# Token products on four array quarters, with one table for the order of all steps, in a recurrent-attention kernel

## The chip, the cores and the metric

The kernel runs on one core of one Trainium2 chip. The metric is the device time of one execution in microseconds (us); smaller is better. A run is called slow when it lies over 1.5% above the fastest of the same kernel on its chip; comparisons use the other runs. The medians quoted below are over all runs, slow ones included.

## The reference

A recurrent attention block gives `y`, and a low-rank token mixer with a channel mixer follows. There are 4 batches, 8 heads, 768 tokens and 40 values to a head.

```python
for t in range(S):                       # state: batch x head x 40 x 40
    y[t]  = einsum('bhd,bhde->bhe', r[t], state)
    Sa    = einsum('bhde,bhe->bhd', state, a[t])
    state = state * w[t] - outer(Sa, b[t]) + outer(v[t], k[t])
x  = y as (batch, token, 8 * 40)
u  = x + transpose(transpose(x) @ U @ V)  # token mixer of rank 32
out = u + maximum(u @ w_ch1, 0) @ w_ch2   # channel mixer, 320 -> 1280 -> 320
```

## The kernel before

The kernel cuts the tokens into 12 chunks of 64. Two batches lie on the two halves of the 128 partitions, so there are 2 x 12 = 24 units of work, each with 8 heads. A unit needs the inverse of a triangular 64x64 matrix for each head. Its 32x32 blocks are eliminated as "lanes" on VectorE or GpSimd, stored to DRAM and fetched back. Then `carry` takes the state from one unit to the next.

In `carry`, batch `x` and head slot `s` (heads `2i` and `2i+1`) name the places on the 128x128 array. An input on partition half `x` whose product is written to half `x` is said to use a diagonal quarter only; the trace before shows these products as 64*64, and 32 of them took 1.01 to 1.06 us (lines 606, 629, 678). The state is kept masked by slot in `ST`, so that a product with 128 input rows can pick it up.

```python
hs = [(i, s, x) for i in range(NP) for s in range(2) for x in range(2)]
for i, s, x in hs:                       # value part: diagonal quarters
    nc.tensor.matmul(out=ph[half(x), s, i], lhsT=u.e[half(x), s, i, :],
                     rhs=vt[half(x), 2 * i + s, 0:D], ...)
for i in range(NP):                      # state part: 128 input rows
    for x in range(2):
        nc.tensor.matmul(out=ph[half(x), :, i], lhsT=u.fa[:, i, half(x)],
                         rhs=ST[:, 2 * i + x, :, 0:D], ...)
# ... the same two kinds again for py, with u.cm and u.fr, and with ng for the token sum ...
for h in range(NH):                      # the state turned: 8 full transposes
    nc.tensor.transpose(out=p[:, h // 4, 128 * (h % 4):128 * (h % 4 + 1)],
                        in_=ST[:, h].rearrange("p s e -> p (s e)"), identity=ID[:])
# ... (cut)
# substitute(): one scratch tile with one buffer, whichever engine eliminates
tmp = qp.tile([128, 240], F32, name="tmp")
GR = [[0, 1], [2, 3]] + [list(range(n, n + 4)) for n in range(4, N, 4)]
# ... (cut) the order: a list LEAD of steps for the start, then a list repeated for every slot,
# with rules such as gathers() and lanes() that issue work when it has become possible
```

## Time and profile before

| | us |
|---|---|
| median of the runs before the prediction | 894.96 (891.09 to 895.43) |
| start, until the first token product of unit 0 | 124.2 |
| middle, the 24 units | 470.9 |
| last stage, the channel mixer | 307.0 |

The stages are read from the profile, which was taken in a run of 903.76 us, 9 us above the median.

The prediction below shows how these stages are read. PE is TensorE, DVE VectorE, ACT ScalarE, POOL GpSimd; "L606" is line 606.

### The profile page before, as it was taken

The numbers are of one execution on the slowest core, as the hardware profiler recorded it, in microseconds if no ns is written. First come the engines' busy times: TensorE is split into PE (matmuls) and PEld (weight loads), VectorE is DVE, ScalarE is ACT, GpSimd is POOL, SyncE is SP. The second block draws the span as 40 slices with busy tenths as digits, with TensorE's granted clock in tenths as the row PEclk, the third lists the DMA queues.
The fourth block names the chain that finished last, engine by engine and source line by source line (L and its number), as shares of the span: only waits on it lengthen the run. The fifth ranks groups of instructions, "written<-read, shape, count | busy, mean of one in ns | idle before, by whom it ended". The sixth has DMA issues, their size and how long they took to land.

```text
span 902.1 us, 27425 instructions
## 1 busy us (share of the span) xinstructions
PE 742.7 (82%) x11914; PEld 546.0 (61%) x11914; DVE 395.5 (44%) x794; ACT 265.1 (29%) x660; POOL 287.3 (32%) x532
## 2 busy tenths in 40 slices
PE   3512285874988989978997999989999999999996
PEld 2412174773977878867886877745546364555544
DVE  5556254552465545556659858731011211112010
ACT  2303042632453535535643535411010000001010
POOL 3323732635367167437749444410000000000000
PEclk9999996977697968979987879989999999999999
DMA  4630444243344444445433543200101000000101
GB/s 63 104 65 1 73 89 85 44 84 66 68 71 78 92 82 81 98 77 90 94 71 74 110 111 83 57 12 1 29 1 29 1 15 15 7 23 1 29 2 32
DMA packets 215265, 49.78 MB, mean 55 GB/s; under 512 B 207617, under 2 KB 210721, under 8 KB 215137
## 3 DMA queue, kind: packets, MB, share of 16 engines
q1 hardware_dynamic: 211968, 47.45, 27.7%
q8 instruction: 96, 1.57, 0.7%
q10 hardware_dynamic: 3168, 0.49, 0.4%
q14 instruction: 33, 0.26, 0.1%
HBM read 37.68 MB, written 10.22 MB: 53 GB/s over the span
## 4 chain that ended last, share of the span: by engine, by line
PE 55%; DVE 8%; DMA 4%; POOL 3%; SPq 2%; issue 2%; ACT 1%; DVEq 0%; POOLq 0%; ACTq 0%
PE p L276 14%; PE p L262 12%; PE p L265 4%; PE ph L606 2%; DMA nT<-td 2%; PE px L589 2%; SPq L335 2%; PE pS L687 2%; PE pe L423 2%; PE ph L611 1%; PE py L629 1%; PE pX L620 1%; PE pv L412 1%; PE py L678 1%; DMA td<-ln 1%
## 5 line engine op out<-in xcount | busy, mean ns | idle before, releaser
L276 PE MATMUL p<-ip,hid 128*128 128x320 f32 x384 | 107.3, 432 | 0.0
L520 POOL TENSOR_TENSOR ln<-ln,tmp 128x30 f32<-128x30 f32 (+19 forms) x180 | 97.0, 539 | 14.1
L518 POOL TENSOR_TENSOR tmp<-ln 128x30 f32<-128x30 f32 (+19 forms) x180 | 92.8, 516 | 23.3 <-DVE ln L520 8.6
L262 PE MATMUL p<-uf,W 128*128 128x512 f32 x200 | 93.7, 612 | 0.0
L267 ACT ACTIVATE hid<-p 128x512 f32<-128x512 f32 x30 | 17.9, 597 | 256.3 <-PE p L265 256.3
L276 PEld LDWEIGHTS p<-ip,hid 128*128 128x128 f32 x384 | 73.0, 190 | 30.4
L268 DVE TENSOR_SCALAR hid<-p 128x512 f32<-128x512 f32 x30 | 20.7, 692 | 126.7 <-PE p L265 126.7
L262 PEld LDWEIGHTS p<-uf,W 128*128 128x128 f32 x200 | 36.9, 192 | 51.9 <-issue 51.1
L469 POOL TENSOR_TENSOR nBT<-nB,ip 128x320 f32<-128x320 f32 x24 | 20.8, 865 | 138.3 <-DVE ip L465 76.9
L279 DVE TENSOR_TENSOR o<-p,XTM 128x320 f32<-128x320 f32 x24 | 11.8, 491 | 117.3 <-PE p L276 117.3
L412 PE MATMUL pw<-ID,nWC 128*128 128x128 f32 x96 | 20.7, 352 | 41.7 <-DVE nWC L437 41.6
L465 DVE RECIPROCAL ip<-ip 128x320 f32<-128x320 f32 x24 | 51.7, 2153 | 0.8
L412 PEld LDWEIGHTS pw<-ID,nWC 128*128 128x128 f32 x96 | 13.7, 177 | 44.1 <-DVE nWC L437 18.3
L423 PE MATMUL pe<-fa,fk 64*64 64x64 f32 x768 | 18.2, 238 | 26.9 <-DVE sn L667 26.0
L428 DVE TENSOR_TENSOR ng<-pg,MU 128x512 f32<-128x512 f32 x24 | 16.5, 688 | 49.2 <-PE pg L423 49.2
L606 PE MATMUL ph<-nV,e 64*64 64x40 f32 x768 | 35.9, 263 | 1.9 <-DVE e L428 1.6
L606 PEld LDWEIGHTS ph<-nV,e 64*64 64x64 f32 x768 | 32.8, 174 | 5.6 <-DVE e L428 2.4
L589 PE MATMUL px<-t,GX 32*64 32x32 f32 x768 | 34.2, 241 | 1.6 <-ACT GX L582 1.6
L412 PE MATMUL pk<-ID,nKT 128*128 128x128 f32 x96 | 15.5, 285 | 24.1 <-POOL nKT L542 24.1
L589 PEld LDWEIGHTS px<-t,GX 32*64 32x64 f32 x768 | 31.0, 159 | 6.8 <-ACT GX L582 4.5
L687 PE MATMUL pS<-ID,ST 128*128 128x128 f32 x176 | 28.1, 311 | 7.8 <-ACT ST L674 3.8
L412 PE MATMUL pb<-ID,nBT 128*128 128x128 f32 x96 | 19.1, 333 | 17.5 <-POOL nBT L469 17.5
(168 smaller groups left out, 1482.8 us busy)
## 6 DMA issues: line engine op xcount, KB each, us to landing
raw<-in_moe_w_ch_dram SPq DMA_DIRECT2D x18, 320.0 KB, 3.1
nR<-in_r_dram SPq DMA_DIRECT2D x48, 80.0 KB, 2.9
nK<-in_k_dram SPq DMA_DIRECT2D x48, 80.0 KB, 2.9
nV<-in_v_dram SPq DMA_DIRECT2D x48, 80.0 KB, 3.0
out_dram<-o SPq DMA_DIRECT2D x48, 80.0 KB, 2.0
nW<-in_w_dram SPq DMA_DIRECT2D x46, 80.0 KB, 3.0
nA<-in_a_dram SPq DMA_DIRECT2D x46, 80.0 KB, 2.8
nB<-in_b_dram SPq DMA_DIRECT2D x46, 80.0 KB, 2.9
```

What stands on the lines that cost most here:

```text
L262: nc.tensor.matmul(out=ps_[x][:], lhsT=W1[i][:, (j + x) * 128:(j + x + 1) * 128], rhs=uf[i], start=(i == 0), stop=False)
L265: nc.tensor.matmul(out=ps_[x][:], lhsT=W1[2][half(x), (j + x) * 128:(j + x + 1) * 128], rhs=uf[2][half(x)], start=False, stop=True)
L276: nc.tensor.matmul(out=p[:, 0:DM], lhsT=hid[:, f, 2 * j * L:2 * (j + 1) * L], rhs=W2[f], start=(f == 0), stop=(f == NJ - 1))
L412: nc.tensor.transpose(out=p[:, 128 * i:128 * (i + 1)], in_=t[:, 2 * i:2 * i + 2, :].rearrange("p h e -> p (h e)"), identity=ID[:])
L423: nc.tensor.matmul(out=p[half(z), s, off + DP * i:off + DP * (i + 1)], lhsT=x[half(s), i, half(z)], rhs=y[half(s), i, half(z)], start=True ...
L465: nc.vector.reciprocal(out=u.ip[:], in_=u.ip[:])
L469: nc.gpsimd.tensor_tensor(out=bt[:, :, 0:D], in0=u.nat["B"][:], in1=u.ip[:], op=ALU.mult)
L518: eng.tensor_tensor(out=x, in0=ln[:, 0:j, j:j + 1].to_broadcast([m, j, n]), in1=ln[:, j:j + 1, j + 1:].to_broadcast([m, j, n]), op=ALU.mult)
L520: eng.tensor_tensor(out=ln[:, 0:j, j + 1:], in0=ln[:, 0:j, j + 1:], in1=x, op=ALU.add)
L589: nc.tensor.matmul(out=px[half(x), 32 * h:32 * h + 32], lhsT=GX[s, h, :], rhs=u.t2[s, h, :], start=True, stop=True)
L606: nc.tensor.matmul(out=ph[half(x), s, i], lhsT=u.e[half(x), s, i, :], rhs=vt[half(x), 2 * i + s, 0:D], start=i + s == 0, stop=first, skip_ ...
L687: nc.tensor.transpose(out=p[:, h // 4, 128 * (h % 4):128 * (h % 4 + 1)], in_=ST[:, h].rearrange("p s e -> p (s e)"), identity=ID[:])
```

## The change

The intent is to shorten TensorE's slot. All token products visit the four quarters in turn: slot 1 writes its output to the other half ("crossed"), so its batches have to be swapped back by two half-tile copies per tile. The state is kept unmasked (`SK`), which removes the masked copies; it is turned by 16 small products. Unit 0's lanes are eliminated alone. A second scratch tile parts VectorE from GpSimd. One table, `ORDER`, fixes the order of every step and the queue of every load. PSUM goes from three single and two double banks (and one for `py`) to two single and three double ones.

```diff
-            for i, s, x in hs:
-                nc.tensor.matmul(out=ph[half(x), s, i], lhsT=u.e[half(x), s, i, :], rhs=vt[half(x), 2 * i + s, 0:D],
+            four = [(i, s, x) for i in range(NP) for s, x in ((0, 0), (1, 1), (0, 1), (1, 0))]
+            for i, s, x in four:
+                nc.tensor.matmul(out=pv[half(x ^ s), s, D * i:D * (i + 1)], lhsT=u.e[half(x), s, i, :],
+                                 rhs=vt[half(x), 2 * i + s, 0:D], start=True, stop=True)
+                for i, s, x in four:
+                    nc.tensor.matmul(out=p[half(x ^ s), s, D * i:D * (i + 1)], lhsT=u.fa[half(s), i, half(x)],
+                                     rhs=state["K"][half(s), i, x, 0:D], start=True, stop=True)
+                nc.vector.tensor_tensor(out=rs, in0=ve[:], in1=p[...], op=ALU.subtract)
   ... (cut: the read of the state with SV, the token sums with ng and cm, likewise)
+        def across(eng, u, t):
+            for x in range(2):
+                eng.dma_start(out=u.x[half(x), 1], in_=t[half(1 - x)])
   ... (cut)
-                for h in range(NH):
-                    nc.tensor.transpose(out=p[:, h // 4, 128 * (h % 4):128 * (h % 4 + 1)],
-                                        in_=ST[:, h].rearrange("p s e -> p (s e)"), identity=ID[:])
+                for i in range(NP):
+                    for x in range(2):
+                        for s in range(2):
+                            nc.tensor.matmul(out=p[half(s), 64 * (2 * i + x):64 * (2 * i + x + 1)],
+                                             lhsT=state["K"][half(s), i, x, :], rhs=ID[half(s), half(s)],
+                                             start=True, stop=True)
   ... (cut)
-        GR = [[0, 1], [2, 3]] + [list(range(n, n + 4)) for n in range(4, N, 4)]
+        GR = [[0], [1, 2, 3]] + [list(range(n, n + 4)) for n in range(4, N, 4)]
-                tmp = qp.tile([128, 240], F32, name="tmp")
+                tmp = qp.tile([128, 240], F32, name="tmp" if eng is nc.gpsimd else "tmpv")
-            return ps.tile([128, 512], F32, name=name, tag="one", bufs=3)
+            return ps.tile([128, 512], F32, name=name, tag="one", bufs=2)
-            return ps.tile([128, 2, 512], F32, name=name, tag="two", bufs=2)
+            return ps.tile([128, 2, 512], F32, name=name, tag="two", bufs=3)
   ... (cut: LEAD, the slot list and their rules go)
+        ORDER = """
+W0 W1a B1x A0 V1a f0 A1x B0x p1 f0 W2x q1 f0 A2 f0 K1x f1 q0 f0 f0 R1x f1 f1 w q0 V2 B2x W3x f1 f2 f1 f0 q1 A3x f2
   ... (cut: 45 more such rows; f, s, c are steps of a unit, W A B V R K loads, g gathers, t fetches, l lanes)
```

## The prediction

> **What bounds the kernel now.** I read the page first (busy shares, the 40 slices), then the three stages by windows, then one undisturbed slot on TensorE (PE), then the waits of the start.
>
> The page's busy shares and two rows of its 40 slices:
>
> ```profile
> PE 742.7 (82%) x11914; PEld 546.0 (61%) x11914; DVE 395.5 (44%) x794; ACT 265.1 (29%) x660; POOL 287.3 (32%) x532
> ...
> PE   3512285874988989978997999989999999999996
> ...
> PEclk9999996977697968979987879989999999999999
> ```
>
> PE is the busiest engine, but it is nearly empty in the first five slices and clocked down in many slices of the middle. So there are three stages: a start until the first token product of unit 0 (it begins at 124 us by the row of line 606, whose 24 uses run from 124.2 to 583.3), the 24 units, and the channel mixer from 595 us on. The windows, with these cuts (columns: stretch, its length, busy us of each engine with its count, granted clock, DMA share, GB/s):
>
> ```profile
> 0.00:124.00 124.00, 44.65 (x452) 35.95 (x452) 66.59 (x145) 24.85 (x66) 51.83 (x127) 1.00 0.38 64
> 124.00:595.00 471.00, 401.98 (x10403) 352.81 (x10402) 282.67 (x571) 218.89 (x558) 235.50 (x405) 0.85 0.42 80
> 595.00:902.10 307.10, 296.06 (x1060) 157.24 (x1060) 46.25 (x79) 21.34 (x36) 0.00 (x0) 0.98 0.06 14
> ```
>
> The last stage is solid PE work that the diff doesn't touch: 307 us stay. The middle is PE-led (402 of 471 us), at a mean clock of 0.85. The start is bound by nobody's capacity: VectorE (DVE), its busiest engine, has 66.6 us of work in 124 us.
>
> One slot that ran at full clock without gaps, on PE (start, us until the group's last end, group); I cost a group by the distance to the next start, because neighbours overlap:
>
> ```profile
> 359.77 1.13 PE L629 MATMUL py<-nKT,cm 64*64 64x40 f32 x32
> 360.83 0.77 PE L634 MATMUL py<-S,fr 128*64 128x80 f32 x16
> 361.54 0.66 PE L417 MATMUL pn<-ID,xf 128*128 128x128 f32 x4
> ...
> 365.92 0.65 PE L423 MATMUL pe<-fa,fk 64*64 64x64 f32 x32
> 366.39 0.84 PE L423 MATMUL pe<-fr,fv 64*64 64x64 f32 x32
> 367.02 1.08 PE L678 MATMUL py<-nBT,ng 64*64 64x40 f32 x32
> 368.03 0.69 PE L578 MATMUL pg<-tt,fh 32*32 32x32 f32 x32
> 368.65 1.09 PE L687 MATMUL pS<-ID,ST 128*128 128x128 f32 x8
> 369.67 1.12 PE L589 MATMUL px<-t,GX 32*64 32x32 f32 x32
> 370.72 1.13 PE L606 MATMUL ph<-nV,e 64*64 64x40 f32 x32
> 371.78 0.77 PE L611 MATMUL ph<-ST,fa 128*64 128x80 f32 x16
> 372.49 0.65 PE L412 MATMUL pv<-ID,nV 128*128 128x128 f32 x4
> ...
> 376.22 0.78 PE L634 MATMUL py<-S,fr 128*64 128x80 f32 x16
> ```
>
> The reader is to see two things. The period, 360.83 to 376.22, is **15.4 us**: the PE floor of a slot. And 32 products of 64x64 that visit all four quarters (line 423) take 0.47 us, while 32 on the diagonal quarters (lines 606, 629, 678: input half x, output half x) take 1.01 to 1.06. The real slot is longer: 23 intervals between 124.2 and about 582.4 us give 19.9 us. The excess of 4.5 us is idle time and low clock: the chain of waits shows line 606's group at 1.86 us several times, against 1.06 here.
>
> Waits within the first 124 us on DVE, and in the middle stage (waiter <- releaser: total, times, longest):
>
> ```profile
> DVE tmp L518 <- POOL ln L520: 19.3, 7, 6.8
> DVE nWC L437 <- DMA nW<-in_w_dram: 11.5, 3, 6.5
> ```
> ```profile
> DVE tt L563 <- DMA nT<-td: 48.3, 10, 14.2
> ```
>
> The first is a false dependence: the elimination of units 0 and 1 on DVE and that of units 2 and 3 on GpSimd (POOL) share one scratch tile "tmp" with one buffer, so the engines take turns. The last is the fetch of eliminated lanes arriving too late for the slot.
>
> [...]
>
> **The change part by part.**
> 1. *Token products, per slot on PE.* Removed: 1.06 (606) + 0.71 (611) + 1.06 (629) + 0.71 (634) + 1.01 (678) + 1.02 (eight full transposes, 687) = 5.57 us. Added: five groups of 32 on four quarters (value part, state part, read of the state, and the two token sums). Such groups cost 0.47 to 0.63 in this slot by what follows; I take 0.58: 2.9 us. The state transpose becomes 16 small products on two quarters, at the 33 ns of line 606: about 0.53, with a switch 0.6. Sum 3.5. The floor falls by 2.1 to **13.3 us**.
> 2. *DVE, per unit.* The slot-masked state copy goes (0.48; its ACT twin of 0.56 goes too), one subtraction comes (0.47). The product with the decay and the final product are halved into two: a 128x8 operation took 0.17 and a 128x320 one 0.50, so a half is about 0.34; that is +0.15 and +0.28 with a second accumulator read of 0.08. Together +0.4 us, 10 us in all. Against it, weight narrowing's last three operations go to POOL for 17 of 27 pieces instead of 13: 4 x 2.0 = 8 us less on DVE, 4 x 2.55 = 10 more on POOL. DVE stays near 12.3 us per slot (282.7/23), POOL near 11. PE still leads, closely.
> 3. *Transfers.* Four more half-tile copies per unit cross the batches (two on ACT's queue, about 0.6 us each of issue). Their results are wanted much later, except the last; off the path. Many loads move to the ACT queue, so the SP queue, which issues some 21 transfers of about 0.55 us per unit, doesn't grow.
> 4. *Start.* Unit 0 is eliminated alone on DVE[...], with its own "tmpv" and "sinkv". I summed the table's steps ahead of the first token product by these durations: 69 us of DVE work, of which the elimination is 21. Add 6 us until the first decay lands and about 10 us of unavoidable waits in unit 0's chain: **85 us** instead of 124.
> 5. *Order.* Fetches, loads and gathers stand apart and earlier, and products are split into short steps so that another group can stand between a product and its eviction. This removes waits, not work. Before, the middle took 471 us for a PE floor of 23 x 15.4 + 12 (the early mixer) = 366, a ratio of 1.29. After, the floor is 23 x 13.3 + 12 = 318. A table that was worked out as a whole should get to about 1.22, not to 1.0, because DVE, POOL and ACT with its issues are nearly as full as PE. 318 x 1.22 = **388 us**.
>
> Sum: 85 + 388 + 307 = 780 us of profiled span. The profile before spans 902.1 against a median of 895.0, so I take off 7: **773 us**.
>
> **The rivals.**
> *A. The clock takes it back.* A less dense PE idles more, and an interval at half clock nearly doubles a group. For it: the clock is already 0.85 with PE 85% busy. [...] If the ratio stays 1.29, the middle is 410 us and the time 795; if the clock falls further, 1.4 and about 830.
> *B. Another engine or the PSUM banks bind.* DVE's 12.3 us plus its waits, or single banks cut from three to two: [...] Also about 795 to 810.
> *C. The table fits nearly perfectly.* Ratio 1.1: 350 us, time 735.
> *D. The start keeps its length*, because unit 0's chain of transfers rather than the scratch tile set it: 30 us more, about 803.
>
> **Range and chances.** Ratios 1.11 to 1.31 with a start of 78 to 98 us give about 738 to 815. Slower than 877 would need both the start and the middle to gain next to nothing. Faster 0.95, same 0.03, slower 0.02.
>
> **What the profile after will show.** First token product near 85 us and no DVE wait on POOL for the scratch tile; groups of 32 token products at about 0.5 us at full clock; slots of about 16 us with PE work of 13.3; a middle clock of at least 0.85; the last stage unchanged at 307. The prediction is wrong if the clock in the middle falls well below 0.8, if a new wait (ACT evictions, SP or ACT issues) opens every slot, or if the four-quarter groups cost 1 us because their neighbours use another tiling.

## More of the kernel before

One more row of the page before turned out to matter, the instruction queue that by the counts further down is TensorE's (packets, megabytes, share of the DMA engines' time):

```profile
q8 instruction: 96, 1.57, 0.7%
```

Each packet has 1.57 MB / 96 = 16 KB (16,384 bytes for every one in the trace). The program has 2 x 11,914 matmuls and weight loads, so a packet holds about 250 TensorE instructions.

## The result and the profile after

The kernel after took **838.83 us**, the median of four runs (829.02 to 845.05); the kernel before took 893.03 beside it. The ratio is 0.931, with a 95% interval of 0.924 to 0.939. A ratio is the mean time of one kernel's fast runs over that of the other's of the same rounds, so it is not quite the ratio of the medians quoted. Two of the four runs after were slow (844 and 845). The direction was right; the time lies 66 us above the predicted 773 and outside the range.

The page of the kernel after, with the rows that answer to those shown of before (busy time and count; 40 slices; instruction packets):

```profile
PE 704.1 (85%) x13146; PEld 504.1 (61%) x13146; DVE 408.0 (49%) x854; ACT 254.3 (31%) x662; POOL 297.2 (36%) x541
...
PE   3653679887888888797898899899999999999996
...
PEclk9965599999988997898779987899999999999999
...
q8 instruction: 105, 1.72, 0.8%
```

TensorE lost 39 us of busy time while its matmuls rose from 11,914 to 13,146. The start is fuller, but the middle still has slices at 7 and 8 tenths, and the clock still dips. The windows, with the same columns as in the prediction:

```profile
0.00:88.40 88.40, 42.83 (x396) 32.17 (x400) 75.31 (x151) 28.78 (x83) 45.11 (x106) 0.76 0.55 93
88.40:524.20 435.80, 368.55 (x11703) 315.82 (x11695) 286.41 (x625) 204.22 (x543) 252.10 (x435) 0.87 0.49 95
524.20:827.30 303.10, 292.76 (x1060) 156.16 (x1060) 46.23 (x79) 21.34 (x36) 0.00 (x0) 0.99 0.06 14
```

The start was shortened by 36 us, nearly as predicted; the last stage is as it was, within 4 us. The middle was to be 388 us and is 436. VectorE, GpSimd and ScalarE are busy for 286, 252 and 204 us of it, so none of them is full. The two waits that the prediction showed are down: VectorE's wait for GpSimd over the scratch tile was 19.3 us in seven times, and its wait for the fetched lanes 48.3 us.

```profile
DVE tmpv L529 <- POOL ln L523: 3.0, 1, 3.0
```
```profile
DVE tt L574 <- DMA nT<-td: 24.8, 9, 4.9
```

What the time of the middle consists of is seen in TensorE's timeline (start, us until the group's last end, group; in brackets the idle time ahead of it and what ended it). The last four rows are from other slots at full clock.

```profile
407.49 0.20 PE L635 MATMUL ps<-SK,fa 64*64 64x40 f32 x1
409.11 0.67 PE L635 MATMUL ps<-SK,fa 64*64 64x40 f32 x31 [1.42 <-issue]
...
412.55 1.13 PE L652 MATMUL pX<-nT,nRH 64*64 64x64 f32 x32
...
417.27 0.63 PE L681 MATMUL pd<-nV,nKT 64*64 64x40 f32 x32
417.71 0.65 PE L681 MATMUL pd<-nx,nBT 64*64 64x40 f32 x32
418.17 0.66 PE L700 MATMUL pg<-nBT,ng 64*64 64x40 f32 x32
418.64 0.65 PE L704 MATMUL pg<-nKT,cm 64*64 64x40 f32 x32
419.11 0.43 PE L624 MATMUL ph<-nV,e 64*64 64x40 f32 x15
421.10 0.54 PE L624 MATMUL ph<-nV,e 64*64 64x40 f32 x17 [1.56 <-issue]
421.57 1.06 PE L597 MATMUL pg<-tt,fh 32*32 32x32 f32 x32
422.57 1.97 PE L717 MATMUL pS<-ID,SK 64*64 64x64 f32 x32
...
450.14 0.69 PE L652 MATMUL pX<-nT,nRH 64*64 64x64 f32 x32
...
457.72 1.10 PE L717 MATMUL pS<-ID,SK 64*64 64x64 f32 x32
458.75 0.69 PE L597 MATMUL pg<-tt,fh 32*32 32x32 f32 x32
459.38 0.68 PE L624 MATMUL ph<-nV,e 64*64 64x40 f32 x32
```

The reader is to see three things. A four-quarter group costs 0.44 to 0.47 us from start to start at full clock, as predicted. Twice, TensorE stops **inside** a group, after 1 of 32 and after 15 of 32 products, for 1.4 and 1.6 us. It waits for no other engine there ("issue"). And soon after each stop the groups take much longer: 1.13 at L652 after the first, 1.06 at L597 and 1.97 at L717 after the second, against 0.69, 0.69 and 1.10 for these groups at full clock.

The trace has the packets of the instruction queue and the granted clock with their times. One packet took from 406.73 to 407.66 us and TensorE resumed at 409.11; another took from 418.70 to 419.66 and it resumed at 421.10: both 1.44 us after the packet's end. The clock was granted at half from 411.14 to 414.56 and from 421.38 to 431.62.

I split the middle of each trace by these records. "Work" is TensorE's busy time less the half-clock excess; the excess is put at half of the busy time that lies in half-clock stretches, an estimate: groups of 8 or 32 that lay wholly in such a stretch took 1.5 to 1.9 times as long as at full clock (L606 before 1.93 against 1.13 us, L624 after 1.04 against 0.66, each group to its last end). A "packet stall" is an idle time over 0.15 us for which the trace shows no releaser and which ends 1.1 to 1.65 us after a packet's end. "Other waits" is the rest of the idle time. The second line of the kernel before is a run of the experiments below that changes its start alone (its scratch tile parted); the second line of the kernel after is a later run of it.

| Middle, us | length | work | half-clock excess | packet stalls (count) | other waits |
|---|---|---|---|---|---|
| before | 470.9 | 348 | 53.5 | 2.3 (4) | 66.7 |
| before, scratch tile parted | 472.3 | 345 | 58.3 | 2.5 (4) | 67.0 |
| after | 435.8 | 316 | 52.8 | 22.4 (25) | 44.9 |
| after, again | 454.3 | 313 | 72.7 | 27.4 (27) | 41.3 |

So work fell by some 32 us and other waits by 22 to 26. Packet stalls gave back 20 to 25 us, and the excess stayed or rose by up to 19. The 18 us between the two runs of the same kernel are nearly all clock.

That the packets cause these stops, and don't merely precede them, is seen by counting TensorE's instructions (matmuls, weight loads and those of its sequencer) in the trace in the order of their starts. All 25 stalls of the kernel after stand 193 or 194 instructions after a multiple of 256, and in each the number of packets that had ended equals that multiple; the same holds for the 4 of the kernel before and for the 45 of `more_many` below. Of the idle times without a releaser in the middle of the kernel after, one alone (0.26 us) is elsewhere. So TensorE stops at the border between two packets of 256 instructions, and no packet's first instruction started less than 1.2 us after that packet's end.

### The profile page after: what moved, and what is told of

Its sections match the earlier page's. It is cut to its first block, busy times and chain, and to the rows that moved or that the text cites. A ratio compares the mean times of both kernels' runs of the same rounds, so it can differ in the third digit from the quotient of the medians.

```text
span 827.3 us, 30102 instructions
## 1 busy us (share of the span) xinstructions
PE 704.1 (85%) x13146; PEld 504.1 (61%) x13146; DVE 408.0 (49%) x854; ACT 254.3 (31%) x662; POOL 297.2 (36%) x541
## 2 busy tenths in 40 slices
DMA packets 241386, 53.87 MB, mean 65 GB/s; under 512 B 233728, under 2 KB 236832, under 8 KB 241248
## 3 DMA queue, kind: packets, MB, share of 16 engines
q8 instruction: 105, 1.72, 0.8%
## 4 chain that ended last, share of the span: by engine, by line
PE 61%; DVE 12%; DMA 9%; POOL 6%; issue 6%; SPq 3%; ACT 2%; ACTq 1%; DVEq 0%; POOLq 0%
PE p L273 16%; PE p L259 13%; PE p L262 4%; PE px L608 3%; PE pS L717 2%; DMA nT<-td 2%; DMA nW<-in_w_dram 2%; PE ps L635 2%; PE pv L202 2%; DVE ip L478 2%; PE pg L597 2%; POOL tmp L529 1%; PE pe L430 1%; PE ph L624 1%; POOL ln L531 1%
## 5 line engine op out<-in xcount | busy, mean ns | idle before, releaser
L531 POOL TENSOR_TENSOR ln<-ln,tmp 128x30 f32<-128x30 f32 (+19 forms) x180 | 96.6, 537 | 14.1
L554 POOL TENSOR_TENSOR nKT<-nK,ip 128x320 f32<-128x320 f32 x24 | 21.6, 902 | 57.0 <-DMA nK<-in_k_dram 29.2
L717 PE MATMUL pS<-ID,SK 64*64 64x64 f32 x704 | 31.9, 249 | 3.9 <-issue 3.3
L608 PE MATMUL px<-t,GX 32*64 32x32 f32 x768 | 30.9, 232 | 3.2 <-ACT ve L630 1.8
L717 PEld LDWEIGHTS pS<-ID,SK 64*64 64x64 f32 x704 | 28.5, 161 | 5.3 <-issue 4.0
L608 PEld LDWEIGHTS px<-t,GX 32*64 32x64 f32 x768 | 27.9, 149 | 5.3 <-ACT ve L630 1.9
L456 DVE TENSOR_TENSOR_SCAN PF<-pw,seg 128x512 f32<-128x512 f32 x24 | 29.4, 1225 | 2.6 <-DVE pw L455 0.5
L419 PE MATMUL pa<-ID,nA 128*128 128x128 f32 x96 | 20.6, 353 | 11.8 <-issue 9.6
L273 PE MATMUL p<-fa,hid 128*128 128x320 f32 x96 | 30.4, 439 | 0.0
L424 PE MATMUL pq<-ID,PF 128*128 128x128 f32 x96 | 18.9, 330 | 12.1 <-DVE PF L456 9.0
L262 PE MATMUL p<-uf,W 64*128 64x512 f32 x100 | 28.2, 641 | 0.0
```

The costliest lines, as they stand in the source:

```text
L262: nc.tensor.matmul(out=ps_[x][:], lhsT=W1[2][half(x), (j + x) * 128:(j + x + 1) * 128], rhs=uf[2][half(x)], start=False, stop=True)
L273: nc.tensor.matmul(out=p[:, 0:DM], lhsT=hid[:, f, 2 * j * L:2 * (j + 1) * L], rhs=W2[f], start=(f == 0), stop=(f == NJ - 1))
L419: nc.tensor.transpose(out=p[:, 128 * i:128 * (i + 1)], in_=t[:, 2 * i:2 * i + 2, :].rearrange("p h e -> p (h e)"), identity=ID[:])
L456: nc.vector.tensor_tensor_scan(out=pf[:, 1:], data0=pw[:], data1=seg[:].rearrange("p h t -> p (h t)"), initial=1.0, op0=ALU.mult, op1=ALU.add)
L531: eng.tensor_tensor(out=ln[:, 0:j, j + 1:], in0=ln[:, 0:j, j + 1:], in1=x, op=ALU.add)
L554: nc.gpsimd.tensor_tensor(out=kt[:, :, 0:D], in0=u.nat["K"][:], in1=u.ip[:], op=ALU.mult)
```

## The experiments

The ratios are to be compared and not the times. Some give wrong results or drop a check, as told.

### The two parts of the change that could be parted

*The scratch tile alone, in the kernel before, and its reverse in the kernel after.*

```diff
-                tmp = qp.tile([128, 240], F32, name="tmp")
+                tmp = qp.tile([128, 240], F32, name="tmp" if eng is nc.gpsimd else "tmpv")
```

> The kernel before, with only the two shared scratch tiles taken apart (VectorE's and GpSimd's scratch of the elimination, VectorE's and ScalarE's sink). Theory A, the false dependence set the start: VectorE's 19.3 us of waits on GpSimd and 8.6 the other way go, the first token product comes at about 105 instead of 124 us, and the time falls by 15 to 25 us to some 872. Rival: the chain of transfers of units 0 and 1 sets the start; then the first token product moves by less than 5 us and the time by less than 1%.

> The changed kernel with the scratch tiles shared again. Theory A: the start goes from 88 to 100 us or more, the time from 834 to about 848. Rival, unit 0 alone and the new order already keep the engines out of each other's way: within 5 us of the changed kernel.

Measured: 883.89 us, ratio 0.985 [0.975, 0.995], with a start of 109.6 us; and 859.01 us, ratio 0.957 [0.948, 0.965], with a start of 96.6 us. In the second, the wait removed came back:

```profile
DVE tmp L529 <- POOL ln L531: 20.5, 4, 9.1
```

The tile is worth 8 to 15 of the 36 us that the start gained. The rest comes from the order and from unit 0's lanes alone, which the next run takes back together. In time the tile is worth 1.5% in the kernel before, less than the 15 to 25 us expected.

*The new steps in the old order* (the old lists and rules, and the old groups of lanes, with the new products and tiles).

```diff
-        GR = [[0], [1, 2, 3]] + ...   and the table ORDER
+        GR = [[0, 1], [2, 3]] + ...   and LEAD, the slot list and their rules of the kernel before
```

> The changed kernel's steps (four-quarter products, crossing copies, separate scratch) put out by the old start list and slot lists, units 0 and 1 eliminated together. It keeps the products and takes back the order. Theory A, in the middle the order is worth nothing and the whole gain there is the 32 us of PE work: the middle is 430 to 445 us, the start 100 to 110, the time about 845 to 860. Rival, the order carried the gain: the middle stays near 470 and the time is 870 or more.

Measured: 965.83 us, ratio 1.078 [1.069, 1.087]; start 120.0, middle 531.8. The work was 312 us, as after, but other waits were 128 us and the excess 86. The costliest waits of TensorE there:

```profile
PE pe L432 <- ACT fh L499: 28.2, 12, 2.4
PE pw L421 <- DVE nWC L446: 14.2, 2, 11.8
PE pX L653 <- DVE nRH L638: 13.0, 4, 10.5
```

Without the table the new products are a loss of 7.8%, and neither reading above foresaw a middle that long. The state part, its subtraction on VectorE and the read of the inverse now stand in a row, and the old order leaves nothing between them; but that wait (`pX` for `nRH`) is 13 of the 128 us, and the rest is spread over many. The old order was made for the old steps, so this run shows that the new steps need an order of their own, not what the order alone is worth. Packet stalls were 5.6 us only: with 128 us of other waits, TensorE mostly had its instructions in time here.

### One engine relieved at a time

These ask whether another engine took over as the bound (the prediction's rival B). Each is the kernel after with one edit.

*No squares on ScalarE* (the range check's accumulators are set to 0).

```diff
-                square(u, key, u.nat[key][:, :, 0:D], 1 / X_HI)
+        nc.gpsimd.memset(SQ[:], 0.0)   # once, at the start
```

> The changed kernel without ScalarE's five range checks a unit (their sums set to zero; the output stays right for these inputs). It takes some 79 us of ScalarE work away, nearly all in the middle. Theory B, the late evictions[...] are what keeps PE idle for 67 us and clocked down for 112 us: the middle falls by 25 us or more, the time below 812. Rivals, transfers, VectorE or the clock by itself: less than 10 us.

Measured: 851.31 us, ratio 0.952 [0.943, 0.961], middle 456.7; no gain. Packet stalls rose to 36 us.

*A cheap operation for VectorE's reciprocal* (wrong result).

```diff
-            nc.vector.reciprocal(out=u.ip[:], in_=u.ip[:])
+            nc.vector.tensor_scalar(out=u.ip[:], in0=u.ip[:], scalar1=1.0, scalar2=None, op0=ALU.mult)
```

> Wrong result on purpose: VectorE's reciprocal (2.15 us a unit) becomes a multiplication by one (about 0.3 us), 44 us of VectorE work less, 34 of them in the middle. If VectorE's chain set the pace of the middle, the time falls by 25 us or more; by theory D (PE's work, packets and clock) it falls by less than 12 us, most of it in the start, where VectorE is the fullest engine.

Measured: 844.08 us, ratio 0.933 [0.923, 0.943]; no gain beyond the spread of the kernel after. (VectorE's operations of the cheap form, on 128x320 values, took 0.26 us at the fastest and 0.32 in the median at line 437 of the kernel before.) Two of its four runs were slow, the profiled one among them, so its trace is not used.

*No crossing copies* (wrong result).

```diff
-                eng.dma_start(out=u.x[half(x), 1], in_=t[half(1 - x)])
+                pass        # and XTM is set to 0.5 at the start
```

> Wrong result on purpose: the four copies a unit that cross the batches are left out (their target is filled once at the start). If the added transfers crowd the queues (issue on ScalarE's queue 1.3 us a unit, 10% more packets), the middle falls by 20 us or more. By theory D they are nearly hidden: less than 10 us.

Measured: 825.75 us, ratio 0.920 [0.912, 0.927], middle 442.2. The kernel after has ratios of 0.931 and 0.941, so the copies cost 1 to 2%, some 10 to 19 us (the lower end is barely clear of the intervals), about 4 of them in the start, which was 83.7 us. They are not free, as I had put it; the page of the kernel after has 12% more DMA packets than that of this run (241,386 against 215,273). Other waits fell to 32 us, but packet stalls rose to 33 and the excess was 62.

*The first crossing on the SP queue instead of ACT's.*

```diff
-            across(nc.scalar, u, qo)
+            across(nc.sync, u, qo)
```

> The changed kernel with the first crossing copies issued from SP's queue instead of ScalarE's (1.3 us of issue a unit taken off ScalarE). By the run without range checks ScalarE has slack, so within 5 us of the changed kernel; if the issue on ScalarE is what delays evictions: 8 us or more faster.

Measured: 849.93 us, ratio 0.948 [0.941, 0.956], against 0.941 [0.934, 0.949] for the kernel after. No difference clear of noise: this gives no sign that it matters which queue issues them.

*Three of four elimination steps on GpSimd left out* (the result stays within the tolerance, but this is no valid elimination; the range flag is set to fine).

```diff
             for j in range(1, LB - 1):
+                if eng is nc.gpsimd and j % 4:
+                    if j % 2 == 0:
+                        yield
+                    continue
```

> The kernel after with three of four elimination steps on GpSimd left out (about 145 us of its 191 us of products and sums; wrong on purpose; the range flag is set to fine). If GpSimd sets the middle stage: a middle of 415 us or less and a time below 825. If it doesn't: within 1.5% of the kernel after, 835 to 855.

Measured: 834.12 us, ratio 0.930 [0.922, 0.937], middle 447.5. GpSimd's busy time in the middle was halved (252 to 127 us) and the middle didn't move; the start fell to 80.6. GpSimd is not the bound.

### More instructions, or more work in few instructions

If TensorE runs short of instructions, the same work must cost more in many small products than in a few wide ones. Both edits stand ahead of the first token product of each unit and add 0.9 to 1.1 us of work to it.

```diff
-            for i, s, x in four:                 # more_many: the value part three times over
+            for i, s, x in four + four + four:
```
```diff
+            for i in range(4):                   # more_few: four wide products, overwritten afterwards
+                nc.tensor.matmul(out=pv[:, 0, 128 * i:128 * (i + 1)], lhsT=ID[:], rhs=ones[:], start=True, stop=True)
             for i, s, x in four:
```

> The changed kernel with the first group of token products issued three times (same output): 128 more PE instructions a unit (64 products with their 64 weight loads), about 1.0 us more of PE at full clock. Theory D: PE's instructions arrive in packets of 16,384 bytes (256 instructions), a packet at best every 3.3 us, so 64 instructions cost 0.83 us and not 0.5. Half a packet more a unit: up to 1.65 us x 24 = 40 us, so the time rises by 25 to 40 us, and the gaps of PE that end 1.2 to 1.6 us after such a packet grow from 22 us to 35 us or more. Rivals (PE's own work, or the clock): at most 24 us, as much as the run with few instructions.

> The counterpart: the same 1.0 us of PE at full clock added at the same place a unit, but in 16 instructions (four full products of 128 columns, in two passes each, whose result is overwritten). Theory D: the packets are nearly as before, so the time rises clearly less than in the run with many instructions: 8 to 20 us; the gaps after packets stay near 22 us or fall. Rival: the same rise in both runs.

Measured: `more_many` 873.65 us, ratio 0.972 [0.962, 0.981]; `more_few` 842.46 us, ratio 0.940 [0.931, 0.949]. Their pages, TensorE's count and the packets, first `more_many`:

```profile
PE 747.7 (85%) x14682; PEld 544.0 (62%) x14682; DVE 405.7 (46%) x854; ACT 255.1 (29%) x662; POOL 294.9 (34%) x541
...
q8 instruction: 117, 1.92, 0.9%
```

and `more_few`:

```profile
PE 717.5 (85%) x13338; PEld 515.1 (61%) x13338; DVE 413.0 (49%) x854; ACT 254.4 (30%) x662; POOL 297.8 (35%) x541
...
q8 instruction: 107, 1.75, 0.9%
```

| Middle, us | length | work | half-clock excess | packet stalls (count) | other waits |
|---|---|---|---|---|---|
| more_many | 480.9 | 338 | 73.1 | 43.9 (45) | 25.4 |
| more_few | 446.2 | 343 | 36.5 | 20.8 (24) | 46.3 |

The work is the same within 5 us, the time differs by 31. With 12 more packets than the kernel after (117 against 105) the stalls rose to 43.9 us from 22 to 27, while other waits shrank: the instructions for the next group had not come when its operands had. With wide products the stalls stayed, the granted clock was 0.92 in the middle (0.84 in `more_many`, 0.87 in the kernel after), and the time rose by at most 8 us (by the ratios) where 8 to 20 were expected. The 35 us between the two middles are 23 of stalls and 37 of half-clock excess, less 21 of other waits and 5 of work. So the larger part of the difference is in the clock's column, in which two runs of the kernel after differ by 20; the pair shows that work costs more in many instructions than in few, but it doesn't part the stalls from a clock that wide products may hold up better.

In the middles of all traces the shortest interval between two packets' starts is 3.2 to 3.5 us, 3.3 in the kernel after. A packet took 1.0 us in the median there. It feeds 256 instructions, that is four groups of 32 products with their loads. At 0.47 us each these last 1.9 us, so by this estimate TensorE outruns its supply in a dense stretch. Where the kernel after took up two packets in a row within 1.65 us of their ends, they lay 3.8 us apart (median of 23). Its middle takes 92 packets: by estimate 304 us at 3.3 and 350 us at 3.8, beside 316 us of work. Before there were 83 packets, 274 and 315 us, beside 348 us of work. Whether the interval depends on the other DMA traffic (busy share 0.49 in the middle) was not tested. The 16 KB of a packet are read from the trace (1.72 MB / 105 packets), and its 256 instructions from the stalls at one place of every 256; why two packets start no closer is not shown.

*Fewer instructions for the turned state*: a third copy in `SK`, and eight full transposes in place of 16 products. The second form moves both halves of its eviction to ScalarE.

```diff
-                        for s in range(2):
-                            nc.tensor.matmul(out=p[half(s), 64 * (2 * i + x):64 * (2 * i + x + 1)], ...
+                        nc.tensor.transpose(out=p[:, w, 128 * i:128 * (i + 1)],
+                                            in_=state["K"][:, i, w:w + 2, :].rearrange("p x e -> p (x e)"),
+                                            identity=ID[:])
```

> The changed kernel with the state transposed by 8 full transposes (16 PE instructions, about 1.02 us) instead of 16 small products in two passes (64 instructions, 1.08 us); the state tile holds its first batch twice (one more VectorE operation of 0.33 us) and the eviction is split between ScalarE and VectorE. Theory D: the run with many instructions paid about 31 us for 112 instructions a unit, so 48 fewer save 8 to 15 us: about 1 to 1.8% faster than the changed kernel, gaps after packets below 20 us. Rival, PE time alone: no change within 4 us, or slower by the added eviction.

> The same with both halves of the eviction on ScalarE. If the packets are what matters: like the run before, within 5 us. If ScalarE's queue is tight: some 10 us worse than with the split.

> The changed kernel unaltered, on the same chip as the next three, for a direct comparison: 829 to 845 us, ratio 0.93 to 0.94.

Measured: 847.01 us (ratio 0.943 [0.936, 0.949]), 846.90 (0.945 [0.940, 0.951]) and, for the kernel after itself, 847.82 (0.941 [0.934, 0.949]). The trace of `turn_full` has four packets fewer in the middle (88), stalls of 22.2 us and other waits of 50.1. The gain of 8 to 15 us that was expected from fewer packets, with stalls below 20, did not come. One more operation on VectorE and a single `SK` buffer stand against the four packets saved, and may have cost what they gave; that is not shown. So this run doesn't bear out a cost in proportion to the instructions.

### The clock

The trace gives the granted clock as 1.0 or 0.5, in stretches of 3.41 us or a multiple. Taking the middle in such windows, I counted TensorE's busy share in each full-clock window by what followed it:

| Full-clock windows | followed by full clock: count, median busy | followed by half clock: count, median busy |
|---|---|---|
| before | 83, 1.00 | 13, 0.55 |
| after | 75, 0.91 | 20, 0.57 |

Windows that were half busy often preceded a fall, but no threshold comes out: after, the windows ahead of a fall were busy for 0.14 to 0.98, and windows from 0.45 up kept the clock. The clock came back only after windows that were at least 0.90 busy (19 cases after, median 1.0; 0.86 in its second trace), but eight windows that were fully busy were still followed by half clock. Before, the clock fell 13 times and stayed down for 11.0 us on average; after, 20 times for 5.6 us. Five of the falls before came at a single idle time of 3.9 to 13.3 us; after, no idle time of the whole middle was longer than 2.9 us.

In the window ahead of the fall there was a packet stall in 1 of 13 cases before, and in 10 of 20 after (13 of 18 in its second trace, 12 of 16 without the crossing copies). Of the windows that kept the clock, 20 of 75 had one too (16 of 69, 28 of 73). So stalls go with falls of the clock more often than without, but this is a coincidence in the traces and not shown by a run: I found no way to take the packets away with nothing else.

Whether filler pays for itself was tried in two places and in the kernel before.

```diff
+            for i in range(4):       # few_at_read: ahead of the read of the inverse; few_twice: there and ahead of ph
+                nc.tensor.matmul(out=p[:, 0, 128 * i:128 * (i + 1)], lhsT=ID[:], rhs=ones[:], start=True, stop=True)
```

> The kernel after with the four wide products only ahead of the read of the inverse, where TensorE waits for VectorE's subtraction: about 27 us of work. Clock as a cause: cold time falls below 110 us and the time stays within 1% of the kernel after. Cost of work: about 870.

> The kernel after with four wide products (128x128 identity against ones) ahead of the first token product and four more ahead of the read of the inverse, all overwritten: about 2.2 us of full-clock work per unit, 53 us in all. If the half clock is a cause of its own: cold time in the middle below 75 us, half-clock excess below 36, and a time within 1.5% of the kernel after (840 to 860). If filler simply costs its work: 53 us more, about 895, with the half-clock excess unchanged at 53 to 73.

> The kernel before with the four wide products ahead of its first token product: about 27 us of work in 23 slots. Clock as a cause: cold time well below the 137 us of before and a time within 1% of it (886 to 904). Cost of work: about 922.

Measured: `few_at_read` 842.75 us, ratio 0.940 [0.935, 0.945]; `few_twice` 839.90, ratio 0.938 [0.934, 0.942]; `before_few` 921.78, ratio 1.027 [1.020, 1.033]. The middle by windows, first of `few_twice`, then of `before_few`:

```profile
90.00:536.30 446.30, 393.70 (x12072) 340.83 (x12071) 283.11 (x622) 202.96 (x539) 250.07 (x433) 0.95 0.48 93
```
```profile
124.40:610.10 485.70, 425.27 (x10587) 373.64 (x10586) 280.85 (x568) 217.27 (x557) 235.27 (x404) 0.87 0.40 77
```

In the kernel after, 55 us of useless work raised the clock from 0.87 to 0.95, cut the excess from 53 to 73 us down to 23, and left the time within its spread. In the kernel before the filler cost about what it took (24 us by the ratio, for 22 us of work), and the excess stayed at 55. There the cost of work came true (922) and the clock's reading missed. My guess, not tested, is that it matters that five of the falls in the kernel before come at single waits of 3.9 to 13.3 us, which four products at another place don't fill.

*Both remedies, and all engines relieved at once* (`relieve_all`: no squares, the cheap reciprocal, no crossing, GpSimd relieved, filler in both places; wrong).

```diff
+ turn_full_few: turn_full with the filler of more_few
+ relieve_all:   few_twice with the edits of no_squares, cheap_recip, no_crossing and pool_less
```

> The kernel after with the state turned by eight full transposes (fewer instructions) and with the four wide products ahead of the first token product. If instruction packets and half clock are the two causes and add up: fewer than 92 packets, cold time near 75 us, and a time 10 us or more below the kernel after, near 830. If not: 840 to 850 as either change alone.

> The kernel after with all reliefs at once: no squares on ScalarE, the cheap reciprocal on VectorE, no crossing copies, three of four GpSimd steps left out, and the filler in two places that keeps the clock up (wrong on purpose). If the engines' joint load sets the middle stage, it comes near TensorE's own work with filler, about 371 us plus the packet stalls of 20, 390 to 410 us in all, and the time near 795. If it is the order and the hand-overs, which none of this touches, or the supply of instructions: a middle of 425 us or more and a time of 815 or more.

Measured: `turn_full_few` 838.71 us, ratio 0.938 [0.934, 0.942]; the two remedies don't add up, and no version with a valid result beat the kernel after beyond its spread. `relieve_all` took 822.23 us, ratio 0.917 [0.910, 0.924]; its middle:

```profile
77.80:516.00 438.20, 390.90 (x12071) 338.75 (x12070) 239.71 (x629) 155.60 (x347) 126.02 (x193) 0.96 0.46 87
```

| Middle, us | length | work | half-clock excess | packet stalls (count) | other waits |
|---|---|---|---|---|---|
| few_twice | 446.3 | 371 | 23.1 | 20.1 (27) | 32.5 |
| relieve_all | 438.2 | 373 | 17.8 | 28.4 (33) | 18.9 |
| turn_full_few | 443.5 | 341 | 36.5 | 12.8 (16) | 53.4 |
| few_at_read | 449.0 | 344 | 40.8 | 24.3 (27) | 40.3 |
| before_few | 485.7 | 370 | 55.4 | 1.9 (4) | 58.5 |

I had read the filler runs as a sign that TensorE no longer sets the middle. `relieve_all` speaks against that: with 47, 43 and 124 us taken from ScalarE, VectorE and GpSimd in the middle, the middle shortened by 8 us. Other waits gave 14 and packet stalls took 8 back. With filler, TensorE's own work, clock and supply fill the middle. What the four reliefs give together without filler was not run, and stays open.

## Why the prediction was wrong

The direction was right and the size was not. Point by point:

- **Start (step 4): right.** 88.4 us came for 85. But the scratch tile is only 8 to 15 us of it; the rest is the order and unit 0's lanes alone.
- **Last stage: right**, 303 to 305 us for 307.
- **Token products (step 1): cost of a group right, saving too large.** The four-quarter groups cost 0.44 to 0.63 us, as said. The term that was mis-sized is the state transpose: 0.6 predicted, 1.03 measured from start to start (457.72 to 458.75 above). I counted the 16 products of the code; the trace shows 32 matmuls for each unit (704 in 22 units), as it does for the token products, which are 16 in the code as well. The eight full transposes of before are eight in the trace. The floor after (318) agrees with the work measured (316) by luck: the floor before (366) was 18 us too high against 348, and the saving was 32 us and not 48.
- **VectorE and GpSimd (step 2): right.** VectorE has 286 us in the middle for 283 before. The step's "PE still leads" holds as well: relieving either gave nothing there.
- **Transfers (step 3): wrong by a little.** The crossing copies were put off the path; they cost 10 to 19 us.
- **Order (step 5): this is the step that failed.** "A table that was worked out as a whole should get to about 1.22." The table did take out waits on other engines: 66.7 to 42-45 us, and the old order with the new products shows that it is needed. But the ratio of the middle to the work was 1.35 before and 1.38 to 1.45 after. I had multiplied the floor by one ratio, as if all excess were waits that an order can remove, and had put what remained down to VectorE, GpSimd and ScalarE; relieving each of them did not shorten the middle. Two parts of the excess are not such waits: the half-clock excess (53 to 58 before, 53 to 73 after) and the packet stalls (2 before, 22 to 27 after). Had these two stayed at 53 and 2, and had the waits come down as they did, the middle would have been 316 + 53 + 2 + 43 = 414 us; the rest of the way to 388 would have taken a clock that recovers.
- **The range:** its lower end doesn't follow from its parts. A ratio of 1.11 with a start of 78 us gives 731, not 738. The measured time lies above the upper end either way.
- **The 7 us from span to median** went the other way: the profile after was taken in the fastest run (span 827.3, medians 838.83 and 847.82), which hides part of the miss.

Of the rivals, A ("the clock takes it back") came nearest with its number, about 830 us, but partly by luck. It wanted a clock below the 0.85 of before, and the middle after was granted 0.87 (0.83 in the second trace); the packet stalls, which no rival named, made the rest. Its half clock lengthened a group by less than double (1.93 against 1.13 us for L606 before). What makes the clock fall was not shown: 5 of the 13 falls before came at a single idle time of 3.9 to 13.3 us; after, the clock fell 20 times with no idle time over 2.9 us. B has the runs that relieved each engine, and all of them, against it (its other half, the PSUM banks, had no run of its own). C and D were not borne out. The list of what would make the prediction wrong named a new wait on an engine; the new wait is on TensorE's own instructions, in the profile under "issue".

## What to carry to other kernels

When small products are spread over the quarters of the array, count instructions as well as time. Here 32 four-quarter products with their loads took 0.47 us, and their 64 instructions, a quarter of a packet, by estimate 0.83 us to arrive (3.3 us between packets at the shortest); the stalls gave back 20 to 25 us of the gain. Stops that always stood at the same place of a packet (193 or 194 instructions after a multiple of 256) gave it away. Split the excess over a floor into work at half clock, waits on others and waits for instructions before scaling it: here the new order with the new products took only the middle one down (66.7 to 41-45 us). And test a suspected clock or supply limit by adding the same work once in many instructions and once in few.
